# Seven products in 45 of the 47 token tiles, and an inverse stage on 64x64 tiles with a re-ordered filter

## The chip, the cores and the metric

The kernel runs on one core of one Trainium2 chip. The metric is device microseconds of that core for one execution, as the median of several runs. The kernel before took 768.46 us (three runs, 767.8 to 769.24).

## The reference

Two layers in a row: a global filter along the sequence (a real Fourier transform, a product with a complex filter, the inverse transform), then a two-layer network with an exact GELU. All inputs and the output are float32.

```python
# x (8, 3008, 256); filt_r, filt_i (1505, 256); w_in (256, 2048); w_out (2048, 256)
X = np.fft.rfft(x, axis=1)
Y = X * (filt_r + 1j * filt_i)[None, :, :]
y = np.fft.irfft(Y, n=3008, axis=1).reshape(8 * 3008, 256)
h = y @ w_in
g = 0.5 * h * (1.0 + erf(h / sqrt(2)))
out = g @ w_out                          # (24064, 256)
```

## The kernel before

The 24,064 tokens are cut into 47 **token tiles** of 512. A token tile has 16 **slots**. A slot holds one block of the first product (`mm1`: 128 of the 2,048 hidden units, two matmuls of 512 columns, then the GELU on ScalarE) and a sixteenth of the second product of the tile before. In some tiles the second product is done plainly, in others with seven products in place of eight: the blocks are combined first by sums on VectorE (`sums_1` to `sums_3`) and the weights once by sums on GpSimd (`weight_sums`).

The Fourier transforms of sequences 1 to 7 (I call them batches) are four **stages** laid between the slots. A sequence of 3008 is 47 x 64, and the stages are products with small tables: s1 (length 47), s2 (length 64) with the filter product, s3 (length 64, back), s4 (length 47, back). Between s1 and s2, and between s3 and s4, the data goes through DRAM (R1 and R2) to change its order. Batch 0 is transformed at the start, by other code, before the first tile.

```python
def s2(self, b, p):                      # two of the 24 k1 at a time
    ps = self.bank("ps_s2")
    for i in range(2):
        k = 2 * p + i
        nc.tensor.matmul(ps[:, 256 * i:256 * i + 256], lhsT=self.T2[:, k]..., rhs=self.st[b, "b", k // 6][:, k % 6, :], ...)
    ...
    nc.scalar.activation(out=p2[0:64], in_=ps[64:128], func=AF.Copy, scale=-1.0)
    nc.scalar.copy(out=p2[64:128], in_=ps[0:64])
    nc.vector.tensor_tensor(out=p1, in0=ps, in1=f(0), op=ALU.mult)
    nc.vector.tensor_tensor(out=p2, in0=p2, in1=f(1), op=ALU.mult)
    nc.vector.tensor_tensor(out=p1, in0=p1, in1=p2, op=ALU.add)

def s3(self, b, p):
    ...
    for i in range(2):
        k = 2 * p + i
        nc.tensor.matmul(ps[:, 256 * i:256 * i + 256], lhsT=self.T3[:, k]..., rhs=w[:, 256 * i:256 * i + 256], ...)
    ...                                  # eviction by VectorE, and from there to R2
def s4(self, b, grp, half):
    ...                                  # one table T4 for all

# ---- cut: the end of the start-up ----
m.load_x(1)                              # GpSimd's queue
m.load_w_out(0)
m.load_w_out(8)
# ---- cut: the schedule, put(slot, what) ----
for b in range(1, B):
    if b == 1:
        s1, n1, r1, s2, n2, r2, s4, n4 = 0, 4, 15, 25, 2.8, 61, 68, 0.72
    ...
    for p in range(12):
        put(s2 + int(n2 * p), m.s2, b, p)
        put(s2 + int(n2 * p) + 4, m.s3, b, p)
put(6, m.weight_sums)
seven = [t for t in range(1, NT - 1) if t % 2 or t > 40]
```

Batch 1 is special. Its stages stand in tiles 0 to 4, right behind the start-up, where x of batch 1 and w_out still arrive. The filter F lies in SBUF, 128 partitions wide, and its rows follow the order in which s2 puts out its results.

Of the kernel before, what the change touches and what calls it, by code (L numbers as in the profile page):

```python
# [10 lines left out]
ALU = mybir.AluOpType  # L11
# [19 lines left out]
class _Mix:  # L31
    def __init__(self, ctx, tc, x, filt_r, filt_i, w_in, w_out, out):
        self.tc, self.nc = tc, tc.nc
        self.x, self.filt_r, self.filt_i = x, filt_r, filt_i
        self.w_in, self.w_out, self.out = w_in, w_out, out
        self.B, self.S, self.D = x.shape
        self.DFF = w_in.shape[1]
        assert self.S == NA * NB and self.D == 256 and self.DFF == 2048
        pool = lambda name, bufs, **kw: ctx.enter_context(tc.tile_pool(name=name, bufs=bufs, **kw))
        P = bass.MemoryType.PSUM  # L40
        self.const = pool("const", 1)
        self.px = pool("px", 1)
        self.pa = pool("pa", 3)
        self.pb = pool("pb", 4)
        self.pp = pool("pp", 4)
        self.pv = pool("pv", 3)
        self.pd = pool("pd", 3)
        self.pool = pool
        self.po = pool("po", 4)
        self.py = pool("py", 1)  # L50
        self.pg = pool("pg", 2)
        self.pq = pool("pq", 1)
        self.small = pool("small", 1)
        self.dram = pool("dram", 2, space=bass.MemoryType.DRAM)
        c = self.const
        self.T1 = c.tile([2 * NA, 96], BF16, name="T1")
        self.T2 = c.tile([128, K1, 2, NB], BF16, name="T2")
        self.T3 = c.tile([128, K1, 2, NB], BF16, name="T3")
        self.T4 = c.tile([96, NA, 2], BF16, name="T4")
        self.T4c = c.tile([96, NA, 2], BF16, name="T4c")  # L60
        self.F = c.tile([128, 2, K1, 256], BF16, name="F")
        self.w_in_sb = c.tile([128, 2, self.DFF], BF16, name="w_in_sb")
        self.w_out_sb = c.tile([128, 16, self.D], FP16, name="w_out_sb")
        self.w_sums = c.tile([128, 4, 8, 128], FP16, name="w_sums")
        self.ps, self.st = {}, {}
        self.flip = 0
# [21 lines left out]
    def load_filters(self, k0, k):  # L88

        nc, D = self.nc, self.D  # L90
        for t, src in enumerate((self.filt_r, self.filt_i)):
            direct = _dram(src, k0 * D, [[NA * D, 32], [D, k], [1, D]])
            mirror = _dram(src, (NA - k0) * D, [[NA * D, 32], [-D, k], [1, D]])
            for q, a in enumerate((direct, mirror)):
                nc.gpsimd.dma_start(out=self.F[32 * q:32 * q + 32, t, k0:k0 + k, :], in_=a)

    def dup_filters(self, eng, k0, k):
        for k in range(k0, k0 + k, 2):
            o, i = (self.F[r:r + 64, :, k:k + 2, :].rearrange("p t a b -> p t (a b)") for r in (64, 0))
            (eng.copy if eng is self.nc.scalar else eng.tensor_copy)(out=o, in_=i)  # L100
# [5 lines left out]

    def load_next(self, b, p, c, h):

        self.gate(self.st[b, "p", p][0:1, 0:1])
        self.load_x(b + 1, 8 * c, 8, (h,))  # L110

    def load_w_in(self):
# [91 lines left out]
    def weights_4(self, g):  # L204

        ts = self.nc.gpsimd.tensor_scalar
        q, self.wt = (g.tile([128, 1], FP32, name=n) for n in ("q48", "wt"))
        ts(out=q, in0=self.p, scalar1=48.0, scalar2=-48.0, op0=ALU.is_ge, op1=ALU.mult)
        self.nc.gpsimd.tensor_tensor(out=q, in0=self.p, in1=q, op=ALU.add)
        ts(out=self.wt, in0=q, scalar1=2.0, scalar2=1.0, op0=ALU.is_ge, op1=ALU.add)  # L210

    def unit_matrices(self, g, cols):
        ts = self.nc.vector.tensor_scalar
# [69 lines left out]
    def table_1_tiles(self, g):  # L283
# [4 lines left out]
        for r in (0, 64):  # L288
            v.tensor_copy(out=self.T1s[r:r + NA, 0:48], in_=self.T1[0:NA, 0:48])

    def s1(self, b, c):

        nc = self.nc
# [10 lines left out]
                                     rhs=x[64 * h:64 * h + NA, w:w + 2, :], start=True, stop=True)  # L304
        for i in range(2):
            for h in range(2):
                self._evac(a[:, h, 2 * i:2 * i + 2, :].rearrange("p a b -> p (a b)"), ps[i][h], False)
        o = self.st[b, "R1"].rearrange("n q c -> q n c")
        for r in range(2):
            for h in range(2):  # L310
# [10 lines left out]
    def s2(self, b, p):  # L321
        nc = self.nc
        ps = self.bank("ps_s2")
        for i in range(2):
            k = 2 * p + i
            nc.tensor.matmul(ps[:, 256 * i:256 * i + 256], lhsT=self.T2[:, k].rearrange("p a b -> p (a b)"),  # L326
                             rhs=self.st[b, "b", k // 6][:, k % 6, :], start=True, stop=True)

        w = self.pp.tile([128, 2, 512], BF16, tag="p12", name="p12")
        p1, p2 = w[:, 0], w[:, 1]  # L330
        f = lambda t: self.F[:, t, 2 * p:2 * p + 2, :].rearrange("p a b -> p (a b)")
        nc.scalar.activation(out=p2[0:64], in_=ps[64:128], func=AF.Copy, scale=-1.0)  # L332
        nc.scalar.copy(out=p2[64:128], in_=ps[0:64])  # L333
        nc.vector.tensor_tensor(out=p1, in0=ps, in1=f(0), op=ALU.mult)  # L334
        nc.vector.tensor_tensor(out=p2, in0=p2, in1=f(1), op=ALU.mult)
        nc.vector.tensor_tensor(out=p1, in0=p1, in1=p2, op=ALU.add)  # L336
        self.st[b, "p", p] = p1


    def s3(self, b, p):  # L340
        nc = self.nc
        if p == 0:
            self.st[b, "R2"] = self.dram.tile([48, NB, 256], BF16, tag="R2", name="R2")
        if p % 2 == 0:
            self.st[b, "v"] = self.pv.tile([128, 4, 256], BF16, tag="v", name="v_sb")
        vt, R2 = self.st[b, "v"], self.st[b, "R2"]
        ps = self.bank("ps_s3")
        w = self.st.pop((b, "p", p))
        for i in range(2):
            k = 2 * p + i  # L350
            nc.tensor.matmul(ps[:, 256 * i:256 * i + 256], lhsT=self.T3[:, k].rearrange("p a b -> p (a b)"),  # L351
                             rhs=w[:, 256 * i:256 * i + 256], start=True, stop=True)
        i = (p % 2) * 2
        self._evac(vt[:, i:i + 2, :].rearrange("p a b -> p (a b)"), ps, False)
        if p % 2 == 1:
            k = 2 * (p - 1)
            o = R2.rearrange("(k r) n c -> (r n) k c", r=2)
            nc.sync.dma_start(out=o[:, k:k + 4, :], in_=vt)

    def r2(self, b, c):  # L360
        d = self.pd.tile([96, 8, 256], BF16, tag="d", name="d_sb")
        self.st[b, "d", c] = d
        R2 = self.st[b, "R2"]
        for g in range(2):
            n = g * HB + c * 8
            self.nc.sync.dma_start(out=d[g * 48:g * 48 + 48, :, :], in_=R2[:, n:n + 8, :])


    def s4(self, b, grp, half):
        nc = self.nc  # L370
        o = b % 2 * self.S
        d = self.st[b, "d", grp // 2]
        ps = self.bank("ps_s4")
        t4 = self.T4.rearrange("p a b -> p (a b)")
        for i in range(4):
            nc.tensor.matmul(ps[:, 94 * i:94 * i + 94],  # L376
                             lhsT=d[:, (grp % 2) * 4 + i, 128 * half:128 * half + 128],
                             rhs=t4, start=True, stop=True)
        yv = self.ring[:, half, o:o + self.S].rearrange("c (m w) -> c m w", w=HB)[:, :, 4 * grp:4 * grp + 4]
        pv = ps[:, 0:376].rearrange("c (i m) -> c m i", i=4)  # L380
        self._evac(yv, pv, False, 1.0 / self.S)



# [230 lines left out]
def kernel(  # L615
# [26 lines left out]
        nc.gpsimd.iota(m.jj[:, lo:lo + 32], pattern=[[sgn * NA, 32]], base=base,  # L642
                       channel_multiplier=0, allow_small_or_imprecise_dtypes=True)
    m.load_x(0, 8, 8, (1,))
    cols = m.iota(g, "cols", [128, 128], [[1, 128]])
    m.load_x(0, 16, 16)
    m.ones = g.tile([128, 512], BF16, name="ones")
    nc.vector.memset(m.ones, 1.0)
# [5 lines left out]
    m.gen_s = m.y0[:, 3072:4608].bitcast(FP32).rearrange("p (k n) -> p k n", n=NB)  # L654
    m.table_2_angle(g, 0)
    m.unit_matrices(g, cols)
    m.T3i = m.pg.tile([128, K1, 2, NB], BF16, tag="g", name="T3i")
    m.vt = m.pg.tile([128, 2, 97, 32], BF16, tag="g", name="vt_sb")
    for k, n in ((0, 4), (4, 8), (12, 12)):
        m.load_filters(k, n)  # L660
# [1 line left out]

    nc.gpsimd.memset(m.vt[:, :, 96, :], 0.0)
    m.dup_filters(nc.gpsimd, 4, 20)


    m.table_2_sin(0)
# [48 lines left out]
            m.warm_up(1)  # L716
            m.c3(11, 1)
    m.warm_up(2)
    m.T1p = g.tile([2 * NA, 2, K1, 2], BF16, name="T1p")
    nc.gpsimd.tensor_copy(out=m.T1p, in_=m.T1.rearrange("p (h r k) -> p h k r", h=2, r=2))  # L720
    m.table_1_tiles(g)
    m.load_x(1)
    m.load_w_out(0)
    m.load_w_out(8)
    m.weights_4(g)

    warm = g.tile([128, 1], FP32, name="warm")
    nc.scalar.activation(out=warm, in_=m.p, func=AF.Gelu)
# [17 lines left out]
    for b in range(1, B):  # L746
        hi = first(b)
        if b == 1:
            s1, n1, r1, s2, n2, r2, s4, n4 = 0, 4, 15, 25, 2.8, 61, 68, 0.72
        else:  # L750
            s1, n1, r1, s2, n2, r2, s4, n4 = hi - 94, 3.5, hi - 80, hi - 69, 3.5, hi - 24, hi - 17, 1
        for u in range(16):
            put(s4 + int(u * n4), m.s4, b, u // 2, u % 2)
        for c in range(4):
            put(s1 + int(c * n1), m.s1, b, c)
            put(r1, m.r1, b, c)
            put(r2, m.r2, b, c)
        for p in range(12):
            put(s2 + int(n2 * p), m.s2, b, p)
            put(s2 + int(n2 * p) + 4, m.s3, b, p)  # L760
        if b + 1 < B:
            for i in range(8):
                put(s2 + int(n2 * (i + 2)), m.load_next, b, i + 2, i // 2, i % 2)

    put(20, m.table_4, m.T4, m.T1p, m.wt, "f", "act")
    put(6, m.weight_sums)
    seven = [t for t in range(1, NT - 1) if t % 2 or t > 40]
    for t in seven:
        for i, s in enumerate((12, 13, 15, 17)):
            put(16 * t + s, m.sums_1, t, 2 * i)  # L770
# [42 lines left out]
```

## Time and profile before

| | before |
|---|---|
| median of runs | 768.46 us |
| profiled span | 766.5 us |
| TensorE (PE) busy | 750.2 us, 98% |
| VectorE (DVE) busy | 551.4 us |
| ScalarE (ACT) busy | 568.2 us |
| GpSimd (POOL) busy | 78.0 us |
| from the start of tile 12 to that of tile 18 (six tiles, about one batch) | 93.50 us |
| start of tile 0 | 39.47 us |
| start of tile 5 | 116.25 us |

The views of the steady stream are in the prediction below.

### The profile page before, as it was taken

What the parts mean: (1) busy time and instruction counts of PE and PEld (TensorE: products, weight loads), DVE (VectorE), ACT (ScalarE), POOL (GpSimd) and SP (SyncE); (2) the same over time, 40 slices, a digit from 0 to 9 for tenths busy, and PEclk for the clock granted to TensorE, in tenths of its full rate; (3) what the DMA queues carried; (4) which work ended last, traced back from release to release, by engine and by line L of the source; (5) the groups of instructions that cost most, each with busy time, mean ns of one, the idle gap of its engine ahead of it and who ended that gap; (6) DMA issues with size and microseconds to landing.
All of it is one profiled execution on the core that took longest, in us unless ns stands there. A gap on an engine that the chain in (4) does not pass through costs nothing.

```text
span 766.5 us, 17837 instructions
## 1 busy us (share of the span) xinstructions
PE 750.2 (98%) x7257; PEld 525.8 (69%) x7257; DVE 551.4 (72%) x1085; ACT 568.2 (74%) x978; POOL 78.0 (10%) x173
## 2 busy tenths in 40 slices
PE   8998999999999999999999999999999999999998
PEld 4846675766777667676777767667677766777776
DVE  8858887586786868768677696767967679636562
ACT  7878955888668875698756986569865788667773
POOL 8751100020000200002000120001100000000000
PEclk9999999999999999999999999999999999999999
DMA  9794645455254662635526456254553422411011
GB/s 153 137 192 108 144 118 129 137 112 146 73 139 116 120 152 63 178 87 109 143 77 178 94 100 163 58 167 100 117 142 81 142 69 84 124 42 43 29 56 57
DMA packets 87284, 85.85 MB, mean 112 GB/s; under 512 B 6689, under 2 KB 77473, under 8 KB 87201
## 3 DMA queue, kind: packets, MB, share of 16 engines
q1 hardware_dynamic: 78816, 68.70, 31.4%
q0 software_dynamic: 8384, 16.00, 14.4%
q8 instruction: 57, 0.93, 0.5%
q14 instruction: 27, 0.21, 0.1%
HBM read 54.00 MB, written 46.66 MB: 131 GB/s over the span
## 4 chain that ended last, share of the span: by engine, by line
PE 86%; DVE 7%; DMA 3%; ACT 2%; POOL 1%; issue 1%; SPq 0%; DVEq 0%; POOLq 0%
PE ps_h L490 39%; PE ps_o L517 19%; PE ps_o L578 19%; PE ps_s L376 2%; PE ps_s L351 2%; PE ps_s L303 2%; PE ps_s L326 2%; DVE s_sb L548 1%; DVE g_sb L554 1%; DMA F<-in_filt_i_dram 1%; ACT g_sb L493 1%; DVE p L334 1%; DVE v_sb L278 1%; DMA x_sb<-in_x_dram 1%; ACT p L332 1%; DVE ost L523 1%
## 5 line engine op out<-in xcount | busy, mean ns | idle before, releaser
L493 ACT ACTIVATE g_sb<-ps_h 128x512 f16<-128x512 f32 x752 | 438.4, 597 | 178.0 <-PE ps_h L490 170.1
L490 PE MATMUL ps_h<-y_sb,w_in_sb 128*128 128x512 bf16 (+3 forms) x1600 | 445.8, 366 | 1.0 <-DVE a_sb L278 1.0
L517 PE MATMUL ps_o<-w_out_sb,g_sb 128*128 128x256 f16 x1392 | 207.3, 273 | 0.0
L517 PEld LDWEIGHTS <-g_sb 128*128 128x128 f16 x1392 | 132.9, 98 | 70.4 <-issue 9.9
L490 PEld LDWEIGHTS <-w_in_sb 128*128 128x128 bf16 x1600 | 138.1, 98 | 15.1 <-issue 1.9
L578 PEld LDWEIGHTS <-g_sb 128*128 128x128 f16 x1600 | 106.0, 98 | 43.7 <-DVE g_sb L554 6.9
L334 DVE TENSOR_TENSOR p<-ps_s,F 128x512 bf16<-128x512 f32 x84 | 57.9, 689 | 63.4 <-ACT p L333 29.6
L578 PEld LDWEIGHTS <-s_sb 128*128 128x128 f16 x1200 | 81.5, 98 | 21.4
L278 DVE CAST a_sb<-ps_s 128x512 bf16<-128x512 f32 x112 | 69.5, 683 | 27.8 <-PE ps_s L303 26.1
L280 DVE TENSOR_SCALAR y_sb<-ps_s 128x376 bf16<-128x376 f32 x112 | 58.8, 544 | 38.6 <-PE ps_s L376 38.2
L578 PE MATMUL ps_o<-w_sums,g_sb 128*128 128x128 f16 x800 | 70.5, 219 | 3.8 <-DVE g_sb L554 3.8
L578 PE MATMUL ps_o<-w_out_sb,g_sb 128*128 128x128 f16 x800 | 66.2, 219 | 3.2 <-DVE ost L523 3.2
L578 PE MATMUL ps_o<-w_sums,s_sb 128*128 128x128 f16 x800 | 69.2, 219 | 0.0
L548 DVE TENSOR_TENSOR s_sb<-g_sb 128x1024 f16<-128x1024 f16 x100 | 65.5, 683 | 2.6 <-ACT g_sb L493 2.6
L105 POOL COPY gate<-p 1x1 bf16<-1x1 bf16 x48 | 13.9, 289 | 447.2 <-DVE p L336 447.2
L278 DVE CAST v_sb<-ps_s 128x512 bf16<-128x512 f32 x84 | 57.3, 684 | 0.9 <-PE ps_s L351 0.8
L332 ACT ACTIVATE p<-ps_s 64x512 bf16<-64x512 f32 x84 | 49.8, 593 | 2.1
L333 ACT CAST p<-ps_s 64x512 bf16<-64x512 f32 x84 | 48.5, 577 | 1.0
L523 DVE COPY ost<-ps_o 128x512 f32<-128x512 f32 x43 | 29.5, 686 | 26.8 <-PE ps_o L517 26.8
L376 PEld LDWEIGHTS <-d_sb 96*128 96x128 bf16 x448 | 30.8, 97 | 25.9 <-DMA d_sb<-R 0.9
L336 DVE TENSOR_TENSOR p<-p 128x512 bf16<-128x512 bf16 x84 | 35.7, 425 | 2.9
L376 PE MATMUL ps_s<-T,d_sb 96*128 96x94 bf16 x448 | 36.3, 204 | 0.4 <-DMA d_sb<-R 0.4
(131 smaller groups left out, 551.7 us busy)
## 6 DMA issues: line engine op xcount, KB each, us to landing
out_dram<-ost SPq DMA_DIRECT2D x93, 256.0 KB, 2.4
x_sb<-in_x_dram POOLq DMA_DIRECT2D x64, 188.0 KB, 3.6
R<-a_sb SPq DMA_DIRECT2D x112, 96.0 KB, 2.1
b_sb<-R SPq DMA_DIRECT2D x28, 384.0 KB, 4.6
R<-v_sb SPq DMA_DIRECT2D x42, 256.0 KB, 2.5
d_sb<-R SPq DMA_DIRECT2D x56, 192.0 KB, 3.9
w_in_sb<-in_moe_w_in_dram POOLq DMA_DIRECT2D x2, 512.0 KB, 9.7
w_out_sb<-in_moe_w_out_dram POOLq DMA_DIRECT2D x2, 512.0 KB, 11.7
```

What stands on the lines that cost most here:

```text
L278: self.nc.vector.tensor_copy(out=out, in_=in_)
L280: self.nc.vector.tensor_scalar(out=out, in0=in_, scalar1=scale, scalar2=None, op0=ALU.mult)
L332: nc.scalar.activation(out=p2[0:64], in_=ps[64:128], func=AF.Copy, scale=-1.0)
L333: nc.scalar.copy(out=p2[64:128], in_=ps[0:64])
L334: nc.vector.tensor_tensor(out=p1, in0=ps, in1=f(0), op=ALU.mult)
L376: nc.tensor.matmul(ps[:, 94 * i:94 * i + 94], lhsT=d[:, (grp % 2) * 4 + i, 128 * half:128 * half + 128], rhs=t4, start=True, stop=True)
L490: nc.tensor.matmul(ps[:, o:o + n], lhsT=self.w_in_sb[:, dc, jc * 128:jc * 128 + 128], rhs=self.ring[:, dc, off:off + n], start=(dc == 0), ...
L493: nc.scalar.activation(out=self.st["g", t][:, jc, :], in_=ps, func=AF.Gelu)
L517: nc.tensor.matmul(ps[:, tile_i % 2, :], lhsT=g[:, jc, tile_i * 128:tile_i * 128 + 128], rhs=self.w_out_sb[:, jc, :], start=(jc == 0), sto ...
L523: nc.vector.tensor_copy(out=ost, in_=ps)
L548: self.nc.vector.tensor_tensor(out=self.st["s", t][:, i:i + 2], in0=a, in1=b, op=ALU.subtract)
L578: nc.tensor.matmul(ps[:, (m + 1) % 2, sub, :], lhsT=a[:, i, 128 * sub:128 * sub + 128], rhs=b[:, i], start=i == 0, stop=i == 7)
```

## The change

The change has four parts. **Seven products** are used in the second product of every tile from 1 to 45 (20 tiles more). **The filter product** becomes one VectorE instruction that multiplies the result of s2 by both halves of the filter; the complex sum is left to s3. **s3** is cut by the parity of k2 into blocks of 64x64, so that four matmuls can run at once on quarters of the array, and the twiddle factors go into one s4 table per column (T4a, made by 24 GpSimd instructions, scheduled from slot 15 on). Half of the evictions move from VectorE to ScalarE. **The filter** has to follow the new order of s2's rows: its first 64 partitions are written to DRAM once and read back re-ordered, in two reloads of eight transfers, one at the end of the start-up (k1 0 to 7, 1 MB) and one in slot 3 (k1 8 to 23, 2 MB). The numbers of buffers change as well (b_sb 3 in place of 4, the products 6 in place of 4, v_sb 2 in place of 3), and so does the spacing of the stages.

```diff
+    def save_filters(self):
+        self.Fd = self.dram.tile([64, 2, K1, 256], BF16, tag="Fd", name="Fd")
+        self.nc.sync.dma_start(out=self.Fd, in_=self.F[0:64])
+
+    def load_filters_again(self, k0, k):
+        for par in range(2):
+            for r in range(2):
+                for q in range(2):
+                    o = 64 * par + 32 * r + 16 * q
+                    self.nc.sync.dma_start(out=self.F[o:o + 16, :, k0:k0 + k, :],
+                                           in_=self.Fd[32 * q + (par ^ q):32 * q + 32:2, :, k0:k0 + k, :])
 ... (cut: the tables T2p, U, T4a and their weights)
     def s1(self, b, c):
-                self._evac(a[...], ps[i][h], False)
+                self._evac(a[...], ps[i][h], "act" if h else False)
     def s2(self, b, p):
-        ... (cut: two ScalarE copies, three VectorE instructions)
+        nc.vector.tensor_tensor(out=w, in0=ps.unsqueeze(1).to_broadcast([128, 2, 512]),
+                                in1=self.F[:, :, 2 * p:2 * p + 2, :].rearrange("p t a b -> p t (a b)"), op=ALU.mult)
-    def s3(self, b, p):
+    def s3(self, b, u):
+        for i in range(2):
+            for t in range(2):
+                for q in range(2):
+                    for par in range(2):
+                        r = slice(64 * par, 64 * par + 64)
+                        nc.tensor.matmul(ps[i][par][64 * q:64 * q + 64, :],
+                                         lhsT=self.U[r, t].rearrange("p r w -> p (r w)"),
+                                         rhs=self.st[b, "p", 4 * u + 2 * i + q][r, t, :], start=t == 0, stop=t == 1)
 ... (cut: s4 with T4a; R2 in another order)
     m.load_x(1)
     m.load_w_out(0)
     m.load_w_out(8)
+    m.load_filters_again(0, 8)
 ... (cut)
-    put(6, m.weight_sums)
-    seven = [t for t in range(1, NT - 1) if t % 2 or t > 40]
+    put(3, m.load_filters_again, 8, 16)
+    put(4, m.weight_sums)
+    put(12, m.table_4_factors, g)
+    put(15, m.table_4_all, g)
+    seven = range(1, NT - 1)
```

## The prediction

> **What bounds the kernel now.** I read the page's busy line first, then the starts of TensorE's matmuls tile by tile, then windows of single tiles, the chain that ended last, and the groups by form.
>
> ```profile
> span 766.5 us, 17837 instructions
> PE 750.2 (98%) x7257; PEld 525.8 (69%) x7257; DVE 551.4 (72%) x1085; ACT 568.2 (74%) x978; POOL 78.0 (10%) x173
> ```
>
> TensorE (PE) is busy 98%, but its records include the drain, so the starts count. In the steady stream a matmul starts 216 ns after one of 512 columns, 109 ns after one of 256 and 56 ns after one of 128; weight loads are hidden. So time is won by streaming fewer columns or by closing gaps. Windows cut at the first GELU of a token tile show the gaps (columns: window; length; busy PE, PEld, DVE, ACT, POOL; clock; DMA share; GB/s):
>
> ```profile
> 240.18:256.73 16.55, 16.55 (x128) 11.71 (x126) 12.33 (x26) 14.97 (x28) 3.00 (x8) 1.00 0.56 119
> 256.73:272.83 16.10, 15.21 (x151) 10.38 (x150) 15.36 (x31) 13.80 (x24) 3.29 (x8) 1.00 0.55 106
> 704.50:717.66 13.16, 13.16 (x148) 9.38 (x146) 8.00 (x18) 9.55 (x16) 0.00 (x0) 1.00 0.12 41
> ```
>
> The last is a pure seven-product tile: 13.16 us, no gap. The middle one is a seven-product tile that also carries the s2/s3 stage: VectorE (DVE) is busy 15.36 of 16.10 us and TensorE has holes. The chain of waits of the same place one batch earlier runs through VectorE, not TensorE (start, length, what):
>
> ```profile
> 162.53 0.60 DVE s_sb L548
> 163.13 0.60 DVE ost L523
> 163.73 0.60 DVE v_sb L278
> 164.33 0.60 DVE p L334
> 164.93 0.34 DVE p L335
> ...
> 165.30 0.42 DVE p L336
> 165.72 0.60 DVE g_sb L554
> 166.32 0.61 DVE s_sb L548
> ```
>
> From the starts, the holes in each of batches 2 to 7 are 0.48+0.24+0.15+0.66+0.12 = 1.65 us. Batch 1 (40 to 103 us) has 1.12 (a_sb waits for its write to memory), 1.46 and 0.95 (VectorE late), 0.33, and 0.57 before s4: 4.4 us.
>
> **What the Trainium skill says.** (1) "TensorEngine Tiling (Array Packing)", Tiling Modes, Key Properties: the 64x64 mode gives four tiles that run in parallel, and changing the mode drains the array. The trace agrees: stage s1 already works so. Its eight 512-column matmuls stand in two groups of four, starting at 124.36 and 124.60; the stream before is held 93 ns and the stream after 92 ns longer than their columns need; the second group starts 240 ns after the first.
>
> ```profile
> 123.83 0.59 PE L490 MATMUL ps_h<-y_sb,w_in_sb 128*128 128x512 bf16 x2
> 124.36 0.63 PE L303 MATMUL ps_s<-x_sb,T1s 47*64 47x512 bf16 x8
> 124.91 0.61 PE L517 MATMUL ps_o<-w_out_sb,g_sb 128*128 128x256 f16 x4
> ```
>
> (2) "VectorE: DVE Perf Modes", Why PSUM operands drop a tier: reads of PSUM lose speed. The trace agrees: 512 f32 elements from PSUM take as long (0.68 us) as 1024 f16 elements in SBUF. (3) "SBUF — State Buffer", Who interferes with whom: a VectorE instruction with two SBUF inputs and a GpSimd (POOL) instruction that reads SBUF lock each other out. The trace agrees: POOL's one-element gate copy takes 0.18 us, but 0.51 when it meets a VectorE sum (at 160.86 it ends at 161.37, just after the sum's 161.33).
>
> **The change, part by part.** The costs come from these groups (instruction, count, busy us and mean ns):
>
> ```profile
> L548 DVE TENSOR_TENSOR s_sb<-g_sb 128x1024 f16<-128x1024 f16 x100 | 65.5, 683 | 2.6 <-ACT g_sb L493 2.6
> L334 DVE TENSOR_TENSOR p<-ps_s,F 128x512 bf16<-128x512 f32 x84 | 57.9, 689 | 63.4 <-ACT p L333 29.6 <-PE ps_h L490 25.1 <-issue 6.2
> L420 DVE TENSOR_TENSOR p<-ps_c,F 128x1024 bf16<-128x1024 f32 x11 | 12.7, 1216 | 0.8 <-POOL F L100 0.6 <-PE ps_c L416 0.2
> L332 ACT ACTIVATE p<-ps_s 64x512 bf16<-64x512 f32 x84 | 49.8, 593 | 2.1
> ```
>
> Back to back, VectorE starts the next instruction some 83 ns before a record ends, so true occupancy is 0.60 us for a 0.68 record, 0.33 for 256 elements, 0.46 for 376, and 1.13 for the 1216 ns form.
>
> *Seven products in 20 more tiles* (even tiles 2 to 40; 25 had it, 45 will). Second product: 64 matmuls x 109 ns = 6.97 us becomes 112 x 55.8 ns = 6.25: 0.72 less each, **-14.4 us** on TensorE. VectorE pays, per tile, eight sums (8x0.60) and eight output steps (8x0.33) for two copies (2x0.60): 7.45 for 1.20 us, so +125 us in all.
>
> *The filter product.* Per pair of k1, L334 + L335 + L336 occupy 0.61+0.40+0.46 = 1.47 us of VectorE, after two ScalarE (ACT) copies of 593 and 577 ns. Now one instruction of the start-up's form: 1.13 us and no copies. 84 pairs: VectorE -28 us, ScalarE -98 us.
>
> *Evictions.* Half of those of s1 (56), s3 (42) and s4 (56) move to ScalarE: VectorE -(56x0.60+42x0.60+56x0.46) = -84 us, ScalarE some +86.
>
> VectorE's sum is +125-28-84 = +13 us occupied: busy some 570 us. What counts is its peak. Now a tile under s2/s3 with seven products asks for 4.57 pairs x (1.47+0.60) + 7.45 = 16.9 us of VectorE against 13.16 + 4.57x0.436 = 15.15 us of TensorE: 1.75 over, which is the measured 1.65 of holes. After: a group of four pairs spans 14 slots; VectorE 4x1.13 + 2x0.60 + 14/16x7.45 = 12.3 us, TensorE 14x0.823 + 8x0.109 + 1.1 = 13.5. That is 91%, in every tile alike. Adding up VectorE's queue slot by slot for the three groups of a batch, the four products are ready when s3 wants them, narrowly in the first. I keep 0.1 us a batch: **-9.3 us**.
>
> *s3 on 64x64 tiles.* Before, 24 matmuls of 256 columns: 24x0.109 = 2.62 us a batch. After, three calls of four groups: 4x0.216 + 3x0.025 + 0.185 for entering and leaving = 1.12, x3 = 3.37. Seven batches: **+5.2 us**, all on TensorE. s2 and s4 keep their matmuls. The R2 writes become 2 KB pieces, the reads 512 B pieces; 12 slots lie between, so they are hidden, except in batch 1.
>
> *Batch 1.* The filters are written once (1.6 MB, near 23 to 30 us, where DMA is almost idle) and read back re-ordered (3.1 MB). The last 2 MB are issued on the same queue after the first s1 call, ahead of the other R1 writes; at some 390 GB/s, the rate of the b_sb loads at 56 to 58 us, they take 5 us. There, from 38 to 47 us, DMA is at 90% or more. The w_out load landed at 47.6 against a first use near 50, and the b_sb loads landed just before the first s2 at 57.5, so 2 to 4 us of waiting appear. GpSimd gains 24 instructions for the s4 table, 0.9 us each by the scale of its 256-element sums (0.63 us): 22 us beside the sums of tiles 1 and 2, some 8 collisions of 0.5 us. VectorE's demand there is 33.5 of 34.7 us, so half or more of that shows. Against them stand VectorE's old 2.4 us of lateness. I put batch 1's holes at 7 us instead of 4.4: **+2.6 us**.
>
> Sum: 766.5 - 14.4 - 9.3 + 5.2 + 2.6 = 750.6 us of span; timed runs are 2 us longer than the span (768.46 against 766.5): **752.5 us**.
>
> **Rivals.** (a) VectorE becomes the bound: at 91% steadily, bunching could make every s3 wait. For it: s3 now wants four products at once, three slots after the last. Against: the queue table above, and steady seven-product tiles need just 8 of 13 us. 0.4 us at each of 21 calls would make 760. (b) The filter reload lies wholly before its need and GpSimd does no harm: batch 1 keeps at most its old 4.4 us, hence 750, or 747 if its VectorE gaps also go. (c) The DMA queue and GpSimd delay batch 1 by 10 us more: 760. For it: the queue is full there already. (d) Four-way overlap fails in s3, and two tiles run at a time: another 12x0.216 us a batch, 18 us in all: 770. Against: s1 shows the overlap with the same shapes and banks.
>
> **Range and chances.** The column terms are safe to a microsecond; batch 1 is open by some 4 us either way and the s3 waits by 3 upwards. So 746 to 760 holds it 8 times in 10. The 2% line is 753.1, just above my number: faster 0.56, within 2% 0.43, slower 0.01.
>
> **What would show it.** Right: stage tiles with VectorE near 90% and no TensorE hole over 0.2 us; every tile without a stage at 13.16 us; s3 as groups of four 240 ns apart, 1.1 us a call; VectorE busy near 570, ScalarE near 556 us. Batch 1's holes before the first second product (w_out), the first s2 (b_sb), and at sums beside GpSimd should come to 7 us. Wrong: holes before each s3 (a), none in batch 1 (b), a start-up moved as a whole (c), s3 calls near 2 us (d).

## More of the kernel before

The two lines are windows of the kernel before, one per tile; the columns are the window, its length, the busy time of PE, PEld, DVE, ACT and POOL with the count of instructions, the granted TensorE clock, the DMA share, and GB/s:

```profile
39.47:50.74 11.27, 10.32 (x63) 4.13 (x62) 9.10 (x15) 8.36 (x17) 4.42 (x7) 1.00 1.09 200
50.74:65.72 14.98, 14.98 (x113) 10.42 (x111) 6.00 (x12) 12.88 (x23) 5.68 (x10) 1.00 0.47 150
```

The reader is to see three things. In the first tile the DMA share is 1.09: the engines' time is wholly taken, by x, w_out and the writes of R1. Yet what they move is 200 GB/s. And TensorE is busy 10.32 of 11.27 us and 14.98 of 14.98, at full clock: nearly all of it arrives in time.

## The result, and the profile after

The changed kernel took **779.02 us** (median of four runs, 777.76 to 782.46), the kernel before on the same chip 768.13 us (four runs). The ratio is 1.0148, with a 95% interval from 1.0112 to 1.0183: inside 2%, but slower, and outside the predicted range. A ratio here is the mean time of one kernel's fast runs over that of the other's of the same rounds, so it isn't quite the ratio of the medians quoted beside it. The output is correct.

The page of the changed kernel, its span and busy times, the shares of the chain that ended last, and two groups of VectorE:

```profile
span 777.8 us, 20180 instructions
...
PE 743.9 (96%) x8388; PEld 520.8 (67%) x8388; DVE 582.1 (75%) x1043; ACT 548.0 (70%) x967; POOL 113.8 (15%) x207
...
PE 80%; DMA 11%; DVE 5%; POOL 2%; issue 1%; ACT 1%; SPq 0%; DVEq 0%; POOLq 0%; ACTq 0%
...
L627 DVE TENSOR_TENSOR s_sb<-g_sb 128x1024 f16<-128x1024 f16 x180 | 121.6, 699 | 0.0
...
L413 DVE TENSOR_TENSOR p<-ps_s,F 128x1024 bf16<-128x1024 f32 x84 | 102.5, 1220 | 16.6 <-PE ps_s L410 15.6
```

TensorE is busy 6 us less, as meant, and the span is 11 us longer. The chain hands DMA 11% of the span, where it was 3%. The two groups are as planned: the filter product is one instruction of 1220 ns, and the sums are there 180 times in place of 100.

Windows of single tiles of the changed kernel, with the columns as before: tile 0, tile 1, a later tile with s2 and s3, and one without a stage.

```profile
39.38:61.90 22.52, 12.77 (x65) 4.82 (x64) 4.15 (x7) 12.46 (x27) 6.37 (x21) 0.85 1.24 166
61.90:90.95 29.05, 17.64 (x112) 11.14 (x111) 7.58 (x7) 9.56 (x16) 16.25 (x23) 0.71 0.63 124
...
189.79:205.14 15.35, 15.35 (x175) 10.69 (x173) 13.97 (x21) 10.60 (x19) 2.87 (x6) 1.00 0.57 117
...
715.76:728.92 13.16, 13.16 (x148) 9.39 (x146) 8.00 (x18) 9.56 (x16) 0.00 (x0) 1.00 0.13 42
```

Tile 0 starts at the same time as before (39.38 against 39.47), so the start-up isn't longer. Then tiles 0 and 1 take 22.52 and 29.05 us in place of 11.27 and 14.98: 25.3 us are lost in two tiles. The granted clock there is 0.85 and 0.71, and matmuls of 512 columns that start 216 ns apart elsewhere start 427 ns apart in the slow stretches (55 to 58 us, and 62 to 79 us with a long wait in between). The stage tile is what the change was made for: TensorE busy 15.35 of 15.35 us, VectorE at 91% beside it. From tile 12 to tile 18 it is 90.62 us, 2.88 less than before.

One number sums it up. Tile 5 starts at 144.82 us, 28.6 later than before. From there to the end it takes 633.0 us, where the kernel before took 650.3: **17.3 us won behind tile 5, 28.6 us lost ahead of it.**

What TensorE waits for in the stretch from 36 to 135 us in the changed kernel (engine, line, released by; us in total, times, longest):

```profile
PE ps_o L596 <- DMA w_out_sb<-in_moe_w_out_dram: 13.5, 2, 11.4
PE ps_t L351 <- ACT a_sb L295: 5.2, 1, 5.2
PE ps_s L455 <- DMA d_sb<-R: 2.4, 1, 2.4
PE ps_s L387 <- DMA x_sb<-in_x_dram: 2.2, 2, 1.1
```

The chain in order of time, at the same place (start, length, what):

```profile
35.82 0.93 POOL w_out_sb L133
37.15 37.42 DMA w_out_sb<-in_moe_w_out_dram
74.61 1.01 PE ps_o L596 x4
```

The second of the two loads of w_out, 512 KB each, is on its way for 37.42 us, and the matmuls of the first second product that need it start when it lands, at 74.6 us. In the kernel before, it had landed at 47.6.

What else is on its way can be seen in the timeline of the sync engine's queue, where the reloads are issued (start, length until the last is issued, queue, line, what, count):

```profile
31.85 4.65 SPq L107 DMA_DIRECT2D F<-Fd  x8
...
41.79 5.01 SPq L396 DMA_DIRECT2D R<-a_sb  x4
...
47.74 6.54 SPq L107 DMA_DIRECT2D F<-Fd  x8
...
56.46 18.59 SPq L396 DMA_DIRECT2D R<-a_sb  x12
```

And in the DMA view of the window from 52 to 68 us (the sum; then each queue with packets, MB and share of the 16 engines' time; then issues with count, KB each and median us to landing):

```profile
DMA packets 693, 2.05 MB, mean 128 GB/s; under 512 B 116, under 2 KB 465, under 8 KB 465
...
q1 hardware_dynamic: 352, 1.87, 103.4%
q0 software_dynamic: 341, 0.17, 13.7%
...
R<-a_sb SPq DMA_DIRECT2D x6, 96.0 KB, 12.0
F<-Fd SPq DMA_DIRECT2D x2, 256.0 KB, 17.4
```

The second reload (queue q1) has the engines' whole time, and brings in 1.87 MB in 16 us: 117 GB/s. An 8 KB packet takes 1.09 us, 7.5 GB/s on one engine; the 3 KB packets of the b_sb loads in the same trace take 121 to 151 ns, some 22 GB/s on one engine. The packets of w_out (q0, 512 B) get in about one for one, 341 beside 352 (112 of the 352 are records of 4 bytes). But that is one for eleven in bytes, 0.17 MB beside 1.87. The R1 writes, behind the reload, take 12 us to land instead of 4.1 (the median at the same place in the kernel before), and the sync queue stands until 75 us.

The 5.2 us line has an earlier cause. The fourth s1 call's evictions wait for an a_sb buffer, that is for the R1 writes of the first call to land; the matmul of the new s4 table, issued right behind, waits for the bank of such an eviction. Those writes stand in the queue behind the *first* reload, whose last transfer lands at 49.5 us; the last of them lands at 54.0, and the wait ends at 54.7. The second reload moves its first packet at 51.7.

### The profile page after: what moved, and what is told of

It reads as the page before. It is cut to its first block, busy times and chain, and to the rows that moved or that the text cites. A ratio compares the mean times of both kernels' runs of the same rounds, so it can differ in the third digit from the quotient of the medians.

```text
span 777.8 us, 20180 instructions
## 1 busy us (share of the span) xinstructions
PE 743.9 (96%) x8388; PEld 520.8 (67%) x8388; DVE 582.1 (75%) x1043; ACT 548.0 (70%) x967; POOL 113.8 (15%) x207
## 3 DMA queue, kind: packets, MB, share of 16 engines
q8 instruction: 65, 1.06, 0.6%
## 4 chain that ended last, share of the span: by engine, by line
PE 80%; DMA 11%; DVE 5%; POOL 2%; issue 1%; ACT 1%; SPq 0%; DVEq 0%; POOLq 0%; ACTq 0%
PE ps_h L569 37%; PE ps_o L657 33%; DMA w_out_sb<-in_moe_w_out_dram 5%; PE ps_s L455 3%; PE ps_s L427 3%; PE ps_s L410 2%; DVE p L413 2%; DMA x_sb<-in_x_dram 2%; PE ps_o L596 2%; PE ps_s L387 2%; DVE s_sb L627 1%; DMA d_sb<-R 1%; DMA F<-in_filt_i_dram 1%; DMA R<-v_sb 1%; DMA R<-a_sb 1%
## 5 line engine op out<-in xcount | busy, mean ns | idle before, releaser
L657 PEld LDWEIGHTS <-g_sb 128*128 128x128 f16 x2880 | 190.9, 98 | 80.4 <-issue 15.2
L657 PEld LDWEIGHTS <-s_sb 128*128 128x128 f16 x2160 | 147.4, 98 | 51.4 <-issue 3.3
L657 PE MATMUL ps_o<-w_sums,g_sb 128*128 128x128 f16 x1440 | 125.6, 220 | 1.2 <-DVE g_sb L633 1.2
L657 PE MATMUL ps_o<-w_sums,s_sb 128*128 128x128 f16 x1440 | 124.5, 219 | 0.0
L627 DVE TENSOR_TENSOR s_sb<-g_sb 128x1024 f16<-128x1024 f16 x180 | 121.6, 699 | 0.0
L657 PE MATMUL ps_o<-w_out_sb,g_sb 128*128 128x128 f16 x1440 | 118.6, 219 | 0.5
L413 DVE TENSOR_TENSOR p<-ps_s,F 128x1024 bf16<-128x1024 f32 x84 | 102.5, 1220 | 16.6 <-PE ps_s L410 15.6
L633 DVE TENSOR_TENSOR g_sb<-s_sb,g_sb 128x1024 f16<-128x1024 f16 x90 | 62.2, 691 | 1.1
L657 PE MATMUL ps_o<-w_out_sb,s_sb 128*128 128x128 f16 x720 | 62.2, 219 | 0.0
L640 DVE TENSOR_TENSOR s_sb<-g_sb 128x1024 f16<-128x1024 f16 x90 | 61.9, 687 | 0.0
L675 DVE TENSOR_TENSOR t_sb<-t_sb,ps_o 128x256 f32<-128x256 f32 x45 | 18.7, 416 | 37.9 <-PE ps_o L657 37.9
L672 DVE TENSOR_TENSOR ost<-t_sb,ps_o 128x256 f32<-128x256 f32 x45 | 18.8, 418 | 31.3 <-PE ps_o L657 31.3
L680 DVE TENSOR_TENSOR ost<-t_sb,ps_o 128x256 f32<-128x256 f32 x90 | 33.5, 414 | 6.8 <-PE ps_o L657 6.8
```

Source lines behind the costliest of these rows:

```text
L413: nc.vector.tensor_tensor(out=w, in0=ps.unsqueeze(1).to_broadcast([128, 2, 512]), in1=self.F[:, :, 2 * p:2 * p + 2, :].rearrange("p t a b ...
L627: self.nc.vector.tensor_tensor(out=self.st["s", t][:, i:i + 2], in0=a, in1=b, op=ALU.subtract)
L633: self.nc.vector.tensor_tensor(out=a21[:, k], in0=self.st["s", t][:, k, 0], in1=a22[:, k], op=ALU.add)
L640: self.nc.vector.tensor_tensor(out=self.st["s4", t][:, k], in0=a12[:, k], in1=s2[:, k], op=ALU.subtract)
L657: nc.tensor.matmul(ps[:, (m + 1) % 2, sub, :], lhsT=a[:, i, 128 * sub:128 * sub + 128], rhs=b[:, i], start=i == 0, stop=i == 7)
L680: v(out=c(h, 1 - h), in0=tt, in1=p, op=ALU.add)
```

## The experiments

The theory after the result: **the second reload, with its narrow transfers, in that place, holds up w_out and R1**, and all the rest follows from it. The rivals: the new GpSimd work delays batch 1; s3 or the seven products are dearer than thought; or the reload is too much traffic wherever and however it is done. Twelve kernels ran, on three chips; the kernel before took 768.04 to 768.29 us (medians) on each, so their medians can be compared.

### Without the second reload (e3_skip)

Its output is wrong, which doesn't matter for the time. Relative error 1.08: most of the filter keeps its old order.

```diff
-    put(3, m.load_filters_again, 8, 16)
```

> The second reload is left out (wrong result on purpose: 16 of 24 k1 use filters in the old row order). Theory A: the best that moving it can give, 750 to 754 us, within 2 us of e1_late. If GpSimd or the first reload or the write of the filters is what costs: 765 or more.

Measured: 760.31 us, ratio to the kernel before 0.9897 (0.9864 to 0.9931), 18.7 us less than the changed kernel by the medians. The reload costs about that, though the 750 to 754 us that I had expected were missed. It isn't all of the 27 us that the changed kernel missed its prediction by: the first reload is still in its place.

### The second reload 13 slots later (e1_late)

```diff
-    put(3, m.load_filters_again, 8, 16)
+    put(16, m.load_filters_again, 8, 16)
```

> Only the issue of the second filter reload (k1 8 to 23, 2 MB) moves, from slot 3 to slot 16, behind the R1 writes and the first three b_sb loads. Theory A (the reload shares the DMA engines with the w_out load packet for packet, w_out packets are 16 times smaller, so w_out lands 27 us late and TensorE waits, then runs at half clock): the w_out waits of 5.4, 2.5 and 11.8 us and the half-clock stretch go, about 752 to 756 us. Rival B (the reload is slow by itself, wherever it stands, and its lateness holds the b_sb loads and s2): still 765 or more. Rival C (GpSimd's table work against VectorE's sums is what costs): stays near 779.

Measured: 762.36 us, ratio 0.9925 (0.9903 to 0.9948), correct. Tile 5 starts at 126.41 us in place of 144.82. The same bytes, in the same transfers, one tile later: nearly all that the reload cost is gone, and the difference from the kernel without it isn't resolved. So it isn't the traffic as such; what it held up mattered. The 752 to 756 us of theory A were missed all the same. A stall of 4.7 us behind the fourth s1 call is left (4.5 in the view of TensorE's waits), and the first reload (35 to 45 us) is what is then ahead of R1:

```profile
PE ps_t L351 <- ACT a_sb L295: 4.5, 1, 4.5
```

### Wider transfers, pattern made at the read (e2_wide)

The place is the change's. Each transfer writes 32 partitions; the order is made by the source pattern, whose outer dimension is the two halves.

```diff
-                for q in range(2):
-                    o = 64 * par + 32 * r + 16 * q
-                    ... F[o:o + 16, :, k0:k0 + k, :] <- Fd[32 * q + (par ^ q):32 * q + 32:2, :, k0:k0 + k, :]
+                o = 64 * par + 32 * r
+                for t in range(2):
+                    src = _dram(self.Fd, par * R + (t * K1 + k0) * 256,
+                                [[(33 - 2 * par) * R, 2], [2 * R, 16], [1, k * 256]])
+                    ... F[o:o + 32, t, k0:k0 + k, :] <- src
```

> The reload stays where the change puts it, but each of its transfers writes 32 partitions (one of the two filter parts) instead of 16 partitions (both parts); same bytes, same packet sizes, same count. If the width of the target is what makes the 8 KB packets take 1.09 us each (7.5 GB/s per engine), the packets take about half, w_out lands some 8 us earlier than its 74.6 and the time falls to about 768 to 772 us. If only place and order count, the same as the change, 779 us.

Measured: 819.72 us, ratio 1.0674 (1.0654 to 1.0695). A miss: 40 us slower than the change, where I had expected it faster. Its DMA view for 68 to 84 us:

```profile
DMA packets 110, 0.85 MB, mean 53 GB/s; under 512 B 6, under 2 KB 6, under 8 KB 6
...
q1 hardware_dynamic: 110, 0.85, 12.6%
```

The packets are quick now (8 KB in 309 ns), but they take 12.6% of 16 engines' time: two engines do it all. The Trainium skill says why, under "DMA: Bandwidth & Descriptors", Why a DMA increments its semaphore by 16 and not by 1: the transfer is spread over the largest k up to 16 that divides the slowest dimension of both patterns. The slowest dimension of this source is 2. The trace agrees: 2 of 16 is 12.5%. So this kernel tested another thing than I meant, and the width was still open.

### Wider transfers, order made at the write (e5_port8)

The order is made when the filters are saved, in two writes between 21 and 32 us. The reload then copies 32 whole rows, and both of its patterns have 32 as the slowest dimension. Bytes, count of transfers and place are the change's.

```diff
     def save_filters(self):
-        self.nc.sync.dma_start(out=self.Fd, in_=self.F[0:64])
+        for q in range(2):
+            dst = _dram(self.Fd, (16 + 32) * R if q else 0, [[R, 16], [-32 * R if q else 32 * R, 2], [1, R]])
+            ... dst <- F[32 * q:32 * q + 32]
     def load_filters_again(self, k0, k):
 ... (cut: the loop over q and its transfer go)
+                o = 64 * par + 32 * r
+                for t in range(2):
+                    ... F[o:o + 32, t, k0:k0 + k, :] <- Fd[32 * par:32 * par + 32, t, k0:k0 + k, :]
```

> Both reloads stay where the change puts them; the rows are put into the new order when they are written to memory, so that a reload transfer writes 32 partitions in a row with the work over all 16 DMA engines (the earlier wide try ran on two engines). If the target's SBUF ports set the rate[...], the 8 KB packets take near 0.55 us instead of 1.09, the 2 MB take 9 to 10 us instead of 17, w_out lands near 60 instead of 74.6, and the time is 763 to 770 us. If the ports don't matter: packets of 1.09 us and 779 us.

Measured: 767.69 us, ratio 0.9993 (0.9976 to 1.001), correct: 11.3 us less than the change by the medians. Its DMA view for 50 to 58 us:

```profile
DMA packets 583, 1.77 MB, mean 222 GB/s; under 512 B 105, under 2 KB 384, under 8 KB 384
...
q1 hardware_dynamic: 302, 1.63, 94.9%
```

The 256 packets of 8 KB take 562 ns in the mean in place of 1043 (1090 in the window above), and 222 GB/s come in, in place of 128. The wait for w_out is 5.66 us in place of 11.8. The Trainium skill has this in "SBUF — State Buffer", Door 1: The DMA port swizzle: partitions 0 to 15 reach four ports, and 104 GB/s were measured there at 1 MiB; 0 to 31 reach eight, and 189 GB/s. This agrees in kind: 117 GB/s for the narrow reload, 204 for the wide one (1.63 MB in 8 us). One thing stays unseparated: this run also reads whole rows of DRAM one after another, where the change reads every other row. That the width does it, and not the order of the read, is argued from the page's figures and not shown; e2_wide, with every other row, took 309 ns a packet, but on two engines only. Where width is named below, the two are meant together. Tile 5 starts at 133.22 us, so place still costs 14 us more than in the next kernel.

### Wide and late, and narrow and late (e6_port8_late, e10_narrow_late)

Both put the first reload in slot 13 and the second in slot 16; e6_port8_late has the wide transfers, e10_narrow_late those of the change.

```diff
-    m.load_filters_again(0, 8)
+    put(13, m.load_filters_again, 0, 8)
-    put(3, m.load_filters_again, 8, 16)
+    put(16, m.load_filters_again, 8, 16)
```

> As e5_port8, and both reloads are issued later (k1 0 to 7 at slot 13, behind the R1 writes; the rest at slot 16, behind the b_sb loads). The first reload was ahead of the R1 writes, and s1's fourth call waits for their landing (4.7 us in e1_late); that should fall to about 1 us: 755 to 758 us. If the 4.7 us come from the x and w_out loads themselves: no faster than e1_late's 762.

> The fourth corner: the 16-partition reloads of the change, at the late places of e6 (slots 13 and 16). Width was worth 11 us at the early place (779 to 767.7) and place 13 us at 32 partitions (767.7 to 754.3). If both work through the same thing, the time for which the reload holds the DMA engines against needed transfers: the narrow reload of k1 0 to 7 now holds the b_sb loads for 8 us instead of 4 and the first s2 waits about 5 us more than in e6: 758 to 762 us. If place alone cures it: 755.

Measured: e6_port8_late 754.30 us, ratio 0.9828 (0.98 to 0.9857); e10_narrow_late 761.18 us, ratio 0.9914 (0.9898 to 0.993). Both are correct. That makes a table of medians:

| us | 16 partitions | 32 partitions |
|---|---|---|
| place of the change | 779.02 | 767.69 |
| slots 13 and 16 | 761.18 | 754.30 |

Each cause is worth something with or without the other: the width 11.3 us in the early place and 6.9 in the late one, the place 17.8 and 13.4. They overlap: less is won by one where the other has been done. That both shorten the same waits is only in part shown: in e10_narrow_late the wait for b_sb ahead of the first s2 is 2.8 us against 0.8 in e6_port8_late, 2 us more where I had expected 5. The stall behind the fourth s1 call is 1.5 us in e6_port8_late, so it was the first reload that made it. Tiles 0 and 1 of e6_port8_late, columns as before:

```profile
40.04:52.23 12.19, 9.95 (x63) 4.03 (x64) 4.15 (x7) 11.72 (x28) 7.00 (x19) 1.00 1.03 198
52.23:68.00 15.77, 14.85 (x110) 10.16 (x111) 7.58 (x8) 9.56 (x18) 15.30 (x20) 1.00 1.01 253
```

They take 12.19 and 15.77 us, 0.9 and 0.8 more than in the kernel before, at full clock. In tile 1 the reloads and the b_sb loads keep DMA at 101% and move 253 GB/s, and TensorE waits for DMA only once there (0.8 us, for b_sb). The slow clock has gone with the stalls; that the stalls brought it on wasn't tested by itself. Tile 5 starts at 118.94 us, 2.7 later than before, where the prediction's terms make it 2.6. The profiled span is 751.3 us, of the fastest of the four runs; the prediction had 750.6.

### The old list of seven-product tiles (e4_late_25)

On the late second reload (e1_late), with seven products in the 25 tiles of the kernel before.

```diff
-    seven = range(1, NT - 1)
+    seven = [t for t in range(1, NT - 1) if t % 2 or t > 40]
```

> e1_late with the old list of 25 seven-product tiles. By the prediction's first term the 20 tiles are worth 0.72 us each: 14.4 us slower than e1_late (about 767 to 770). If VectorE's extra load eats part of it: less than 10 us slower.

Measured: 774.31 us, ratio 1.0071 (1.0047 to 1.0095), against 762.36 for e1_late. The 20 tiles are worth 12.0 us by the medians, 11.2 by the ratios, where 14.4 were predicted. In the trace tiles 12 to 17 take 92.57 us in place of 90.62; three of the 20 tiles lie there, so 0.65 us for each in place of 0.72. From tile 5 to the end it is 644.7 against 632.3 us, 0.66 for each of 19. The runs of e1_late alone spread from 760.44 to 763.98 us, so I don't lean on the last 2 us of the medians.

### Every s3 matmul twice (e12_s3_twice)

On e6_port8_late; the second pass overwrites the first with the same values.

```diff
-            for t in range(2):
+            for t in (0, 1, 0, 1):
```

> As e6_port8_late, with every s3 matmul done twice (the second pair starts the sum anew, so the result is right). If four 64x64 tiles run at a time and s3 lies wholly on TensorE's path, the 84 added groups of four cost 0.216 + 0.025 us each: 20 us slower than e6, about 774. If only two tiles run at a time: 36 us or more. If s3 is partly hidden beside waits: well under 18 us.

Measured: 770.54 us, ratio 1.0041 (1.002 to 1.0061), 16.2 us over e6_port8_late, correct. One batch takes 93.21 us, 2.59 more: 12 groups of four more at 0.216 us are 2.59. So four matmuls do run in the time of one, and s3 has no spare time around it in the steady stream. My 20 us for the whole was too much; six batches make 15.5, and batch 1, which has holes, shows only about one more.

### Fewer table instructions on GpSimd (e7_no_t4)

On e6_port8_late, with 6 of the 24 instructions for T4a, and zeros elsewhere (relative error 0.81). Its output is wrong, which doesn't matter for the time.

```diff
-        for w in range(0, HB, 8):
+        self.nc.gpsimd.memset(self.T4a, 0.0)
+        for w in range(0, 8, 8):
```

> As e6_port8_late, but GpSimd makes only a quarter of the s4 table (6 of 24 instructions, the rest zeros: wrong result on purpose). Theory: GpSimd's two-input sums lock VectorE's two-input sums out (their mean is 1.01 to 1.31 us in 64 to 92 us of e1_late, 0.68 later). Then they fall to 0.68 us there, and the time falls by 3 to 5 us against e6_port8_late. If VectorE is late there for its own load: under 1 us.

Measured: 753.59 us, ratio 0.9817 (0.9798 to 0.9836), 0.7 less than e6_port8_late. That isn't resolved. VectorE's sums between 60 and 92 us are a little shorter with fewer GpSimd instructions beside them (779 ns in the mean of eight, against 924), so the lock can be seen in the records, but it doesn't reach the end.

### Half of the table ahead of the weight sums (e8_split_t4)

On e6_port8_late, to use GpSimd while w_out is still on its way.

```diff
 ... (cut: table_4_all is given the columns to make)
-    put(4, m.weight_sums)
-    put(12, m.table_4_factors, g)
+    put(6, m.table_4_factors, g)
+    put(7, m.table_4_all, g, (0, 8))
+    put(8, m.weight_sums)
-    put(15, m.table_4_all, g)
+    put(15, m.table_4_all, g, (16, 24))
```

> As e6_port8_late, with the right result: half of the s4 table is made on GpSimd while it would wait for w_out (slots 7 to 8), ahead of the weight sums; the other half afterwards. Half of the collisions go: 1.5 to 3 us faster than e6_port8_late, unless the weight sums now come too late for the first seven-product tile, which would show as TensorE waiting for w_sums near slot 36.

Measured: 757.01 us, ratio 0.9851 (0.9834 to 0.9868): 2.7 us slower than e6_port8_late by the medians. The intervals overlap, so that it is slower isn't resolved; the 1.5 to 3 us of gain were missed. Timelines of VectorE and of GpSimd in this kernel (start, length, engine, line, what, count):

```profile
62.81 6.09 DVE L630 TENSOR_TENSOR s_sb<-g_sb 128x1024 f16<-128x1024 f16 x2
```

```profile
62.85 2.55 POOL L616 TENSOR_TENSOR w_sums<-w_out_sb,w_sums 128x256 f16<-128x256 f16 x4
65.35 1.62 POOL L374 TENSOR_TENSOR t_sb<-t_sb 96x376 f32<-96x376 f32 x2
67.05 1.31 POOL L376 TENSOR_TENSOR T4a<-t_sb 96x376 bf16<-96x376 f32 x1
```

Of the two VectorE sums, the first lasts 4.71 us (62.81 to 67.52); it takes 0.68 alone. GpSimd's instructions stand back to back all that time, and the sum gets in about where GpSimd, whose next instruction needs the result of the one before, leaves a gap of 78 ns (66.97 to 67.05). TensorE's longest wait follows from there: 3.4 us for VectorE's output step, which stands in VectorE's queue behind the sum. After it the granted clock is at half from 70.6 to 77.4 us, which it never is in e6_port8_late before the end. That the wait alone makes the 2.7 us is argued, not shown.

### s4 of batch 1 two slots later (e9_s4_later), and the reloads later still (e11_both)

e9_s4_later is e6_port8_late with s4 of batch 1 from slot 70, in smaller steps. e11_both is e9_s4_later with the reloads in slots 16 and 19.

```diff
-            ... r2, s4, n4 = ..., 62, 68, 0.72
+            ... r2, s4, n4 = ..., 62, 70, 0.6
```

```diff
-    put(13, m.load_filters_again, 0, 8)
+    put(16, m.load_filters_again, 0, 8)
-    put(16, m.load_filters_again, 8, 16)
+    put(19, m.load_filters_again, 8, 16)
```

> As e6_port8_late, with batch 1's s4 begun two slots later (70 instead of 68, at 0.6 slots a step instead of 0.72, so that it still ends at slot 79). In e6 TensorE waits 2.3 us for d_sb before the first s4. If that wait is only the distance to the R2 read: 1 to 2 us faster, about 753 us. If the two slots only move the wait to the last quarter of s4 (its d_sb is read later): no difference.

> As e9_s4_later, with the 32-partition reloads behind the b_sb loads (slots 16 and 19). TensorE's wait of 1 us for b_sb before the first s2 should go, if the first products do not then wait for the filters: 0.5 to 1.5 us faster than e9_s4_later.

Measured: e9_s4_later 752.86 us, ratio 0.9804 (0.9788 to 0.9821), correct. It is the fastest of all and beats both kernels. The wait for d_sb ahead of the first s4 is 1.31 us in place of 2.28; against e6_port8_late the intervals overlap, so a gain of about 1 us is likely and not certain. e11_both took 756.62 us, ratio 0.9848 (0.9833 to 0.9862): a miss. Now the filter comes too late: VectorE's filter product waits 4.2 us for it. Of the places tried slots 13 and 16 are the best, with w_out and R1 on one side and the first filter product on the other.

## Why the prediction was wrong, point by point

**Seven products: held.** A tile without a stage takes the predicted 13.16 us. The mechanism was right and the size a little off: the trace gives 0.66 us for a tile where 0.72 was put, the runs 12.0 us in all (11.2 by the ratios) where 14.4 was.

**The filter product and the evictions: held.** The one instruction is 1220 ns long, VectorE is busy 582.1 us (some 570 predicted), ScalarE 548.0 (some 556). The 1.65 us of holes a batch are 0.23 now (0.1 predicted). In the steady stream VectorE at 91% is the bound of nothing, so rival (a) is out there. One reading in the prediction was off: by their starts the three old instructions occupy 0.61, 0.45 and 0.34 us, 1.40 in all and not 1.47, so 22 us were saved there and not 28; that is half of the 12 us by which VectorE is busier than predicted. And the comparison made for reads of PSUM is of f32 with f16, so it doesn't separate where an operand lies from its type; no run here does.

**s3: held.** Three calls a batch at 1.07 us, where 1.12 was put. In the timeline of TensorE in the changed kernel, the 16 matmuls of one call take 1.06 us by their records, with the stream going on behind:

```profile
178.84 1.06 PE L427 MATMUL ps_s<-p,U 64*64 64x512 bf16 x16
179.83 0.51 PE L657 MATMUL ps_o<-w_sums,g_sb 128*128 128x128 f16 x6
```

The groups of one call start 240, 216 and 216 ns apart, and e12_s3_twice adds them at 216. Rival (d) is out. A batch is shorter by 2.88 us; the terms made it about 3.0 (three tiles at 0.72 and 1.55 us of holes less, 0.75 of s3 more). Behind tile 5 the terms make 18.5 us (19 tiles, six batches), and 17.3 were won; 0.66 in place of 0.72 a tile is the difference.

**Batch 1: failed, and nearly the whole miss is here.** The term was +2.6 us. Ahead of tile 5 the prediction made the change 2.6 us dearer in sum: there is one new seven-product tile (0.72 less) and s3 of batch 1 (0.75 more) in it besides, and these nearly cancel. It was 28.6 dearer, so the term itself is 28.5; that is 26 of the 27 us by which the span was missed. The step that failed is the sentence on the last 2 MB: "at some 390 GB/s, the rate of the b_sb loads at 56 to 58 us, they take 5 us". They took some 18 us, from about 52 to 70, at 117 GB/s (the issue view above has 17.4 us to landing for the last two transfers). I carried the rate of a load of 128 partitions over to transfers of 16 partitions. "2 to 4 us of waiting" became 2.47 and 11.82 us ahead of the first second products, and matmuls took 0.21 us longer each in the stretches of slow clock. w_out wasn't merely queued in a busy system: its packets took turns with packets that each ran for 1.09 us.

A second step failed with it: the reload at the end of the start-up was never priced. It runs from about 35 to 49 us and keeps x (two waits of 1.1 us), the issue of w_out (GpSimd waits 2.7 us) and R1 back (5.35 us behind the fourth s1 call). In e1_late, where the second reload is out of the way, a stall of 4.7 us is still there. The write of the filters was put at 23 to 30 us, "where DMA is almost idle"; in the kernel before DMA is full there until about 25 us, and the write took from 22 to 32.

By TensorE's starts the 28.6 us can be shared out. Ahead of tile 5 the waits of over 0.3 us come to 26.8 us, against 4.1 in the kernel before; matmuls at the slow clock lose some 5.8 us more.

**GpSimd: not resolved.** I put about 2 us; e7_no_t4 finds 0.7 with an interval wider than that. e8_split_t4 shows that the lock can cost more where GpSimd works without a gap.

**The rivals.** Rival (c) named the right place, DMA and GpSimd in batch 1, and the right sign, with 10 us where some 27 were missing; DMA carried nearly all of it, as far as e7_no_t4 can tell on e6_port8_late. Rival (b), that batch 1 loses nothing, is out. The mechanism was in my text, then, and its size was off by a factor of three in rate, which is the difference between a transfer that hides and one that doesn't. With that cured (e6_port8_late) the span is 751.3 us against the predicted 750.6, and the holes of batch 1 that I could count add up to some 7 us, where 7 had been put. That agreement is in part luck: the median is 754.30 us against 752.5 predicted, and of the holes 2.3 us wait for d_sb ahead of s4 and 1.5 for a_sb, where the prediction looked to w_out and b_sb.

What stays open is what sets the slow clock off, whether width or the order of the read makes the reload faster, and the last 2 us of the seven-product term.

## What to carry to other kernels

Price a transfer from a measured one of the same shape: the same partitions written, the same split of its patterns over the engines; a rate taken from a 128-partition load was three times too high for 16 partitions here. Ask of each new transfer what small load it will share the engines with, and whether that load is the one that the next matmul waits for: moving the same bytes by a tile was worth more than halving their time. Where an order has to be changed through DRAM, make it in the write that has time, and let the read that is waited for be plain and wide.

## What the Trainium skill lacked or had wrong

- "SBUF — State Buffer", Door 1: The DMA port swizzle: it gives rates for a range of partitions, but not what one packet takes, which is what a small load beside it waits for. A packet of 8 KB took 1043 ns in the mean where 16 partitions are written, 562 ns where 32 are, and 309 ns while only two engines were at work.
- "DMA: Bandwidth & Descriptors", Queues, rings and completion order: it says that an engine takes turns between queues packet by packet, and the trace agrees in kind (352 records beside 341). It lacks what that does to a load in small packets: the 512 B packets of w_out moved 0.17 MB while the 8 KB packets of the reload moved 1.87, and one load of 512 KB took 37.4 us, where 11.7 us is the median of the two in the kernel before.
- "SBUF — State Buffer", Who interferes with whom: the engine that comes second is said to block for the other's instruction; it lacks what happens when such instructions follow without a gap. Here a VectorE sum of 0.68 us took 4.71 us beside GpSimd instructions of 0.67 to 0.84 us each that stood back to back; the wait was over six of them, until a gap of 78 ns.
